# K Qᵀ and K S as one 112-column product, and two small products moved to other visits, in a DeltaNet + SwiGLU kernel

## The chip, the cores and the metric

The kernel runs on one core of one Trainium2 chip. The metric is the device time of one execution in microseconds, the median of several runs. The engines are TensorE (PE, with its weight loads listed as PEld), VectorE (DVE), ScalarE (ACT), GpSimd (POOL) and SyncE (SP), which issues most DMAs. All numbers are fp32.

## The reference

Two blocks follow each other. The first is a DeltaNet recurrence over 768 steps for 4 batches of 8 heads with a head dimension of 48; its output, 3072 rows of 384, goes through a SwiGLU feed-forward block with 1536 hidden columns.

```python
k_n = k / (norm(k) + 1e-6)
state = zeros(B, H, D, D)
for t in range(S):
    y[:, :, t] = einsum('bhd,bhde->bhe', q[:, :, t], state)
    v_old = einsum('bhde,bhd->bhe', state, k_n[:, :, t])
    state = state + beta[t] * einsum('bhd,bhe->bhde', k_n[:, :, t], v[:, :, t] - v_old)
x = y.transpose(0, 2, 1, 3).reshape(B * S, H * D)
g = x @ w_gate
out = (g * sigmoid(g) * (x @ w_val)) @ w_out
```

## The kernel before

The 768 steps are cut into 12 chunks of 64. Inside a chunk the recurrence is a handful of matrix products per head, with the state S (48 x 48 a head) carried from chunk to chunk. For chunk c they are, in order: the grams K Kᵀ and K Qᵀ (64 x 64 a head), r = V − K S, u = Z r with Z the inverse of a triangular matrix made from K Kᵀ, the new state S + Kᵀ u, and the output y = Q S + P u with P the masked K Qᵀ. The feed-forward block of chunk c runs while the recurrence of chunk c+1 is worked off between its products.

There are 32 heads (4 batches x 8). For each product TensorE runs 32 matmuls, one a head; `every()` walks over the heads so that four successive ones fall on the four 64x64 quadrants of the array: the row half by the head's parity `par`, the column half by the batch half `b` and `par`. Each matmul leaves two records in the trace (64 for a product). The results lie in two pairs of PSUM banks, `px` and `py`; the feed-forward products use four other banks, `ffn`.

All engines run in an order written out by hand. The feed-forward block of a chunk (`gate_val_fast`, three rounds, then `output_fast`) calls `point(c + 1)` at fixed places; each such visit does one thing for the recurrence: a step of `join`, a step of `products` (`turned`, that is the transposed K and Q, then in another visit the `gram`), or a step of `advance`. After a visit `fill(n)` gives VectorE some steps of the triangular inversion (`invert`) of a later pair of chunks, as many as fit in the budget n less what the visit has used up (`spent`). `finish` works off whatever is still due at the end of a chunk; `may_advance` says when a chunk's first step may be taken.

`advance(c)` for a chunk from 2 on has four steps, each a visit:

- the r visit: K S into `px` (L918), Q S into `py` (L927), then VectorE subtracts K S from V (L935);
- the u visit: u into `px` (L957), ScalarE copies it out (L969);
- the P u visit: Kᵀ u into `px` (L1025), VectorE adds it to the state (L1034), P u is added onto Q S in `py` (L1013), ScalarE copies y out (L1070, L1072);
- the transposes of y (L1086) and a copy to `x_ffn` (L1092).

The grams (L521) are made in a visit of their own: K Kᵀ in `px`, copied out by ScalarE (six copies, L547 and L550), K Qᵀ in `py`, masked by VectorE (L539). K runs some four chunks ahead of the recurrence, Q one chunk. From K chunk 6 and Q chunk 3 on, the transposes are done by VectorE (L494) from blocks that SP loads (`load_blocks`, L173).

Of the kernel before, what the change touches and what calls it, by code (L numbers as in the profile page):

```python
# [20 lines left out]
def kernel(  # L21
# [25 lines left out]
    nc = tc.nc  # L47

    B, H, S, D = q.shape
    NCH = S // C  # L50
    NJ = H // 2
    NB = B // 2
# [9 lines left out]
    const = ctx.enter_context(tc.tile_pool(name="const", bufs=1))  # L62
# [11 lines left out]
    def ps_pair(name, tag):  # L74

        return pairs_of_banks[tag]
# [35 lines left out]
    def kt_of(c):  # L112
        return kts[c] if c < AHEAD else kts_late[c % 4]
# [202 lines left out]
    nc.vector.memset(half, 0.5)  # L316

    spare = const.tile([128, 1], FP32, name="spare")
    nc.scalar.activation(spare, half[:, 0:1], ACTF.Silu)
# [154 lines left out]
    def banks(name, tag):  # L474

        if type(tag) is int:
            return [ps_ffn([128, 512], name, tag + i) for i in range(2)]
        p = ps_pair(name, tag)
        return [p[:, 0], p[:, 1]]

    def turned(c, of_q, tag=None):

        if tag is None:
            tag = "py" if of_q else "px"
        x = qpad[c % QB] if of_q else kn_of(c)
        if of_q:
            xt = work.tile([128, NB * NJ * 2 * C], FP32, name="qt", bufs=1)
        else:
            xt = kt_of(c)
        if c >= blocks_of[of_q][1]:  # L490
            xt_v = xt.rearrange("p (b bp j i) -> p bp j b i", bp=NB, b=2, j=NJ)
            (qt if of_q else kt)[c] = xt_v
            blocks = blocks_of[of_q][2]
            nc.vector.transpose(xt, blocks.rearrange("p bp h d -> p (bp h d)"))  # L494
# [4 lines left out]
        xt = xt.rearrange("p (bp j b i) -> p bp j b i", bp=NB, j=NJ, b=2)  # L499
        (qt if of_q else kt)[c] = xt  # L500
        p_t = banks("p_t", tag)
        for bp in range(NB):
            for j in range(NJ):
                at = slice(128 * j, 128 * j + 128)
                nc.tensor.transpose(p_t[bp][:, at], x[:, bp, 2 * j : 2 * j + 2], ident)
            if type(tag) is int:
                nc.scalar.copy(xt[:, bp].rearrange("p j b i -> p (j b i)"), p_t[bp])
        for bp in range(NB if type(tag) is not int else 0):
            nc.scalar.copy(xt[:, bp].rearrange("p j b i -> p (j b i)"), p_t[bp])
        if of_q and c + QB < Q_BLOCKS:  # L510
            load_q(c + QB)

# [42 lines left out]
    def gram(*args):  # L555
        for _ in gram_steps(*args):
            pass
# [348 lines left out]
    def advance(c):  # L906
# [4 lines left out]
        if c > 0 and c not in scaled:  # L911
            scale_v(c)
        r = vin.pop(c)
        if c > 0:
            p_y = recur(ps_pair("p_y", "py"))
            p_r = recur(ps_pair("p_r", "px"))
            for bp, j, par, b, first in every():
                nc.tensor.matmul(  # L918
                    p_r[half_of(b ^ par), par, bp, j],
                    kt[c][head_of(par), bp, j, b],  # L920
                    state[head_of(par), b, bp, j],
                    start=first,
                    stop=True,
                    skip_group_check=True,
                )
            for bp, j, par, b, first in every():
                nc.tensor.matmul(  # L927
                    p_y[half_of(b ^ par), par, bp, j],
                    qt[c][head_of(par), bp, j, b],
                    state[head_of(par), b, bp, j],  # L930
                    start=first,
                    stop=False,
                    skip_group_check=True,
                )
# [76 lines left out]
        def p_of_u():  # L1011
            for bp, j, par, b, _ in every():
                nc.tensor.matmul(  # L1013
                    p_y[half_of(b ^ par), par, bp, j],
                    pq[half_of(b), par, bp, j],
                    uu[half_of(b), par, bp, j],
                    start=False,
                    stop=True,
                    skip_group_check=True,
                )  # L1020
# [21 lines left out]
                    else:  # L1042
                        late_loads.append(lambda: load_k(c + 2))

        if 0 < c < NCH - 1:
            of_state()
        y = work.tile([128, NB, NJ, 2, D], FP32, name="y", tag="r", bufs=2)
        if c == 0:
            third = single(2)[0]
            for par in range(2):  # L1050
                for bp in range(NB):
                    p = third if par and bp else p_y[par]
                    for j in range(NJ):
                        for b in range(2):
                            nc.tensor.matmul(
                                p[half_of(b ^ par), bp, j],
                                pq[half_of(b), par, bp, j],
                                uu[half_of(b), par, bp, j],
                                start=j == 0 and (bp == 0 or par == 1),
                                stop=True,  # L1060
                                skip_group_check=True,
                            )
                if par == 0:
                    nc.scalar.copy(y[:, :, :, 0], p_y[0])
            for b in range(2):
                nc.scalar.copy(y[half_of(b), 0, :, 1], p_y[1][half_of(1 - b), 0])
                nc.vector.tensor_copy(y[half_of(b), 1, :, 1], third[half_of(1 - b), 1])
        else:
            p_of_u()
# [286 lines left out]
    def minus(out, a, b):  # L1356
        nc.vector.tensor_tensor(out=out, in0=a, in1=b, op=ALU.subtract)
# [159 lines left out]
    def steps(kind, *args):  # L1517
        return gens.get((kind, args), (None, 0))[1]

    fills = []  # L1520
    inverted, joined1 = set(), []

    def products(k_c, q_c):

        if k_c is not None:
            turned(k_c, False)
        if q_c is not None:
            turned(q_c, True)
        yield
        if k_c is not None:  # L1530
            gram(k_c, False, None, (nc.scalar.copy, nc.scalar.copy))
            if k_c % 2 == 1:
                fills.append((k_c // 2, invert(k_c // 2)))
        if q_c is not None:
            gram(q_c, True)
        yield
# [30 lines left out]
    def prep_step(c):  # L1567

        for g in range(1, c // 2 + 2):
            late = g == 1 and (  # L1570
                hold or steps("join", g) >= 2 and steps("advance", 2) < 4
            )
            if g in inverted and steps("join", g) < (4 if g == 1 else 2) and not late:
                step("join", join if g > 1 else join_1, *((g,) if g > 1 else ()))
                return True
        if going:
            next(going.pop())
            return True
# [8 lines left out]
        next(gen)  # L1587
        going.append(gen)
        return True

    def point_and_fill(c, n, fill):
# [208 lines left out]
```

## Time and profile before

| | |
|---|---|
| median of 3 runs | 698.48 us (698.16 to 700.41) |
| span of the profiled execution, first to last instruction | 694.1 us |
| median less span | 4.4 us |
| TensorE busy | 680.5 us, 98% |
| VectorE busy | 473.1 us, 68% |
| ScalarE busy | 259.8 us, 37% |
| mean granted TensorE clock | 0.997 |

The profile gives no device time of its own for the profiled execution, only the span; the median is 4.4 us above it, for what lies around the first and the last instruction. A line such as L918 is that line of the kernel before. In the timeline each row is a start, a length, the engine, the line and the operation, with the number of merged records; matmuls are pipelined, so the length of a group holds the drain of its last record, and what a group costs is read from the start of the next one.

### The profile page before, as it was taken

Reading aid. Unit: us, or ns where it says so; the run is one execution under the profiler, and the core shown is the slowest. Engines: PE = TensorE matmul, PEld = TensorE weight load, DVE = VectorE, ACT = ScalarE, POOL = GpSimd, SP = SyncE. Lnnn points to the kernel's source line nnn. Section 1 sums busy time; section 2 is a strip of 40 time slices with the busy share of each in tenths; the row PEclk is TensorE's granted clock in tenths of the full one; section 3 lists DMA queues with packets and bytes.
Section 4 is the critical chain, followed back from the end, with each engine's and each line's share of the span. In section 5 each row is a group of like instructions: output and inputs, shape, how many; then the busy total and the mean of one; then the engine's idle time right before and its main releaser. Section 6 shows DMA issues by size and latency. Waiting matters only on the chain.

```text
span 694.1 us, 25652 instructions
## 1 busy us (share of the span) xinstructions
PE 680.5 (98%) x11380; PEld 635.6 (92%) x11380; DVE 473.1 (68%) x1104; ACT 259.8 (37%) x549; POOL 53.5 (8%) x62
## 2 busy tenths in 40 slices
PE   8799999999999999999999999999999999999997
PEld 4688888757999999999999999999999999999997
DVE  6887779798899758896469786389844345333342
ACT  4674776214442532344233244242153142142230
POOL 5110031105000030000300002100000000000000
PEclk9999999999999999999999999999999999999999
DMA  9567924017550621564432363243241231221210
GB/s 136 148 167 180 275 69 161 1 34 174 133 109 16 117 79 40 103 116 84 94 72 70 73 135 70 56 108 70 55 108 48 58 83 46 55 63 46 69 47 23
DMA packets 143854, 62.31 MB, mean 90 GB/s; under 512 B 122976, under 2 KB 126048, under 8 KB 143744
## 3 DMA queue, kind: packets, MB, share of 16 engines
q1 hardware_dynamic: 141536, 60.19, 37.0%
q8 instruction: 89, 1.46, 0.9%
q10 hardware_dynamic: 2080, 0.39, 0.4%
q0 software_dynamic: 128, 0.10, 0.1%
q14 instruction: 21, 0.17, 0.1%
HBM read 53.58 MB, written 7.08 MB: 87 GB/s over the span
## 4 chain that ended last, share of the span: by engine, by line
PE 90%; DMA 4%; SPq 3%; ACT 1%; issue 1%; DVE 1%; POOL 0%; ACTq 0%; POOLq 0%; DVEq 0%
PE ffn L1193 43%; PE ffn L1399 20%; PE ffn L1289 8%; PE ffn L1316 4%; DMA h_f<-in_moe_w_val_dram 3%; PE p_px L957 2%; PE p_px L918 2%; PE p_py L1013 2%; SPq L140 1%; PE p_py L927 1%; PE p_py L521 1%; PE p_px L1025 1%; PE p_px L521 1%; SPq L186 1%; PE p_py L1086 1%; DMA wo_sb<-in_moe_w_gate_dram 1%
## 5 line engine op out<-in xcount | busy, mean ns | idle before, releaser
L1193 PE MATMUL ffn<-x_ffn,wg_sb 128*128 128x128 f32 x840 | 128.3, 275 | 0.3 <-ACT x_ffn L1092 0.2
L1193 PE MATMUL ffn<-x_ffn,wv_sb 128*128 128x128 f32 x840 | 128.1, 275 | 0.0
L1193 PEld LDWEIGHTS ffn<-x_ffn,wg_sb 128*128 128x128 f32 x840 | 111.1, 192 | 0.6 <-ACT ffn L1249 0.3
L1193 PEld LDWEIGHTS ffn<-x_ffn,wv_sb 128*128 128x128 f32 x840 | 110.7, 192 | 0.0
L1223 ACT ACTIVATE sil<-ffn 128x256 f32<-128x256 f32 x120 | 46.1, 384 | 131.8 <-PE ffn L1193 127.1
L1399 PE MATMUL ffn<-wo_sb,h_f 128*128 128x192 f32 x480 | 83.4, 327 | 0.0
L1228 DVE TENSOR_TENSOR h_f<-sil,ffn 128x256 f32<-128x256 f32 x120 | 49.5, 418 | 47.7 <-ACT sil L1223 45.2
L1399 PEld LDWEIGHTS ffn<-wo_sb,h_f 128*128 128x128 f32 x480 | 78.1, 190 | 0.4
L1360 DVE TENSOR_TENSOR ffn<-ffn,p_sb 128x512 f32<-128x512 f32 x58 | 40.4, 696 | 44.1 <-ACT ffn L1249 43.0
L1193 PE MATMUL ffn<-x_t,h_f 128*128 128x128 f32 x480 | 61.1, 280 | 0.0
L1193 PEld LDWEIGHTS ffn<-x_t,h_f 128*128 128x128 f32 x480 | 56.2, 191 | 1.4 <-ACT ffn L1206 0.2
L599 DVE TENSOR_TENSOR zb<-zb,tmp 128x31 f32<-128x31 f32 (+15 forms) x155 | 53.1, 342 | 5.3
L593 DVE TENSOR_TENSOR tmp<-zb,mb 128x31 f32<-128x31 f32 (+15 forms) x155 | 52.6, 339 | 4.0
L826 POOL TENSOR_TENSOR n_b<-mb,half 128x32 f32<-128x32 f32 x5 | 30.0, 6003 | 289.2 <-DVE mb L563 289.2
L1360 DVE TENSOR_TENSOR o_sb<-o_sb,ffn 128x192 f32<-128x192 f32 x49 | 17.2, 351 | 51.2 <-PE ffn L1399 49.1
L1206 ACT COPY ffn<-ffn 128x512 f32<-128x512 f32 x30 | 17.1, 571 | 63.5 <-PE ffn L1193 57.1
L1399 PE MATMUL ffn<-last_k,h_f 128*128 128x192 f32 x200 | 35.9, 327 | 0.0
L1289 PE MATMUL ffn<-x_ffn,wg_sb 128*128 128x256 f32 x144 | 34.4, 385 | 0.0
L1289 PE MATMUL ffn<-x_ffn,wv_sb 128*128 128x256 f32 x144 | 33.8, 382 | 0.0
L1399 PEld LDWEIGHTS ffn<-last_k,h_f 128*128 128x128 f32 x200 | 32.9, 190 | 0.0
L1289 PEld LDWEIGHTS ffn<-x_ffn,wg_sb 128*128 128x128 f32 x144 | 26.5, 190 | 4.3 <-DVE wg_sb L309 0.7
L1289 PEld LDWEIGHTS ffn<-x_ffn,wv_sb 128*128 128x128 f32 x144 | 27.0, 190 | 3.7
(302 smaller groups left out, 1064.3 us busy)
## 6 DMA issues: line engine op xcount, KB each, us to landing
h_f<-w_s SPq DMA_DIRECT2D x60, 256.0 KB, 2.9
p_sb<-w_s SPq DMA_DIRECT2D x27, 256.0 KB, 2.7
vin<-in_v_dram SPq DMA_DIRECT2D x48, 96.0 KB, 3.2
out_dram<-o_sb SPq DMA_DIRECT2D x48, 96.0 KB, 2.2
kn<-in_k_dram SPq DMA_DIRECT2D x20, 192.0 KB, 4.7
zt<-in_moe_w_out_dram SPq DMA_DIRECT2D x6, 384.0 KB, 3.7
qpad<-in_q_dram SPq DMA_DIRECT2D x36, 64.0 KB, 3.2
w_s<-h_f SPq DMA_DIRECT2D x7, 256.0 KB, 4.1
```

Source lines behind the costliest of these rows:

```text
L521: nc.tensor.matmul(p_v[par][half_of(b if of_q else b ^ par), bp, j], kt[c][half_of(par), bp, j, b], xt[half_of(par), bp, j, b],)
L593: nc.vector.tensor_tensor(out=t_v, in0=zb[:, 0 : j + 1, j : j + 1].to_broadcast([128, j + 1, m]), in1=mb[:, j : j + 1, j + 1 : R].to_broad ...
L599: nc.vector.tensor_tensor(out=zb[:, 0 : j + 1, j + 1 : R], in0=zb[:, 0 : j + 1, j + 1 : R], in1=t_v, op=ALU.add,)
L826: nc.gpsimd.tensor_tensor(out=n, in0=mb.rearrange("p j i -> p (j i)")[:, 0 : R * R : R + 1], in1=half, op=ALU.pow,)
L1193: nc.tensor.matmul(p[:, u], w(u), moving, start=start and u == 0, stop=True, skip_group_check=True,)
L1206: nc.scalar.copy(p_y, p_x)
L1223: nc.scalar.activation(sil[:, n].rearrange("p (i n) -> p i n", i=2), p[:, 0:2], ACTF.Silu)
L1228: nc.vector.tensor_tensor(out=h_of(c, f, j), in0=sil[:, n].rearrange("p (i n) -> p i n", i=2), in1=p[:, 2:4], op=ALU.mult,)
L1289: nc.tensor.matmul(ps[name][:, i], w_sb[:, t, (f + i) * 128 : (f + i + 1) * 128], xts[c][:, t], start=(t == 0 and i == 0), stop=(t == KT - 1),
L1316: nc.tensor.matmul(p_o, hs[c, f - f % 2][:, f % 2, bp * 128 : (bp + 1) * 128], wo_sb[:, f], start=(f == 0), stop=(f == FT - 1),)
L1360: nc.vector.tensor_tensor(out=out, in0=a, in1=b, op=ALU.add)
L1399: nc.tensor.matmul(p[x, part], a(f - f % 2)[:, f % 2], b(f), start=not begun and f == 0, stop=f == FH - 1, skip_group_check=True,)
```

## The change

From chunk 4 on (`FUSED = 4`) Q is turned into the same tile as the state: `qs` has 16 slots of 112 columns, 64 of Qᵀ and 48 of the state. The r visit then makes K Qᵀ and K S in one product of 112 moving columns with Kᵀ stationary; a head's parity decides whether it lands in `px` or `py`. VectorE takes K S off V in two halves and masks K Qᵀ in three pieces. Q S is made at the beginning of the P u visit; behind it ScalarE copies two elements of its result to `spare_2`. K Kᵀ of chunks 7 to 11 (`K_LATE = 7`) is made in `py` in the u visit of whichever chunk comes next. The visits that held only grams are gone from chunk 4 on; `may_advance` asks for the turned Q instead of the masked P. Before chunk 4 the products stay as they were, with the state and Qᵀ now views of `qs`.

```diff
-    state = const.tile([128, 2, NB, NJ, D], FP32, name="state")
+    qs = const.tile([128, B * NJ, C + D], FP32, name="qs")
+    state = qs[:, :, C : C + D].rearrange("p (b bp j) d -> p b bp j d", b=2, bp=NB)
+    q_part = qs[:, :, 0:C].rearrange("p (b bp j) i -> p bp j b i", b=2, bp=NB)
+    FUSED, K_LATE = 4, 7
+    waiting_k = []
...
+            if of_q:
+                qt[c] = q_part
+                nc.vector.transpose(
+                    qs[:, :, 0:C], blocks.rearrange("p (h i) -> p h i", i=C)
+                )
...
+        if c >= FUSED:
+            both = [
+                [p.rearrange("p (j n) -> p j n", j=NJ) for p in row]
+                for row in (
+                    [bank[:, 0 : NJ * (C + D)] for bank in banks("p_r", tag)]
+                    for tag in ("px", "py")
+                )
+            ]
+            for bp, j, par, b, _ in every():
+                nc.tensor.matmul(
+                    both[par][bp][half_of(b ^ par), j],
+                    kt[c][head_of(par), bp, j, b],
+                    qs[head_of(par), NB * NJ * b + NJ * bp + j],
+                )
...
+            for par in range(2):
+                minus(r[:, par], r[:, par], pair[par][:, :, :, C : C + D])
...
+            for to, of, par in (
+                (slice(0, 128), slice(0, 128), 0),
+                (half_of(0), half_of(1), 1),
+                (half_of(1), half_of(0), 1),
+            ):
+                rows = of.stop - of.start
+                nc.vector.tensor_tensor(
+                    out=p_sb[c][to, par],
+                    in0=pair[par][of, :, :, 0:C],
+                    in1=mask_q[of, None, None, :].to_broadcast([rows, NB, NJ, C]),
+                    op=ALU.mult,
+                )
+            spent.append(3.3)
+            yield
+        elif c > 0:
...
         uu = v0
+        if c >= FUSED and waiting_k:
+            k_gram(waiting_k.pop(), "py")
...
-        if 0 < c < NCH - 1:
+        if 0 < c < FUSED:
             of_state()
...
         else:
+            if c >= FUSED:
+                p_y = recur(ps_pair("p_y", "py"))
+                q_of_state(p_y)
+                nc.scalar.copy(spare_2, p_y[:, :, 0, 0, 0:1])
+                if c < NCH - 1:
+                    of_state()
             p_of_u()
...
+        if k_c is not None and k_c >= K_LATE:
+            waiting_k.append(k_c)
+            k_c = None
+        if q_c is not None and q_c >= FUSED:
+            q_c = None
+        if k_c is None and q_c is None:
+            return
         yield
...
-        return steps("advance", c) > 0 or (c in p_sb and steps("join", g) >= due)
+        ready = c in qt if c >= FUSED else c in p_sb
+        return steps("advance", c) > 0 or (ready and steps("join", g) >= due)
```

`q_of_state` is the old loop over L927 as a function, `k_gram` the old call of `gram` for K with the start of its inversion.

More of the change, by code (lines that the diff above doesn't have):

```diff
@@ L318 @@
     spare = const.tile([128, 1], FP32, name="spare")
+    spare_2 = const.tile([128, 2, 1], FP32, name="spare_2")
     nc.scalar.activation(spare, half[:, 0:1], ACTF.Silu)
@@ L485, in turned @@
         x = qpad[c % QB] if of_q else kn_of(c)
[L486 to L489, printed above, removed]
+        xt = None if of_q else kt_of(c)
         if c >= blocks_of[of_q][1]:
[L491 to L494, printed above, removed]
+            blocks = blocks_of[of_q][2].rearrange("p bp h d -> p (bp h d)")
+            if of_q:
[3 more added lines that the diff above has]
+                )
+            else:
+                kt[c] = xt.rearrange("p (b bp j i) -> p bp j b i", bp=NB, b=2, j=NJ)
+                nc.vector.transpose(xt, blocks)
             spent.append(1.8)
@@ L498, in turned, with copy_turned @@
             return
-        xt = xt.rearrange("p (bp j b i) -> p bp j b i", bp=NB, j=NJ, b=2)
+        if of_q:
+            xt = q_part
+        else:
+            xt = xt.rearrange("p (bp j b i) -> p bp j b i", bp=NB, j=NJ, b=2)
         (qt if of_q else kt)[c] = xt
         p_t = banks("p_t", tag)
+        def copy_turned(bp):
+            if of_q:
+                p = p_t[bp].rearrange("p (j b i) -> p j b i", j=NJ, b=2)
+                nc.scalar.copy(xt[:, bp], p)
+            else:
+                nc.scalar.copy(xt[:, bp].rearrange("p j b i -> p (j b i)"), p_t[bp])
         for bp in range(NB):
@@ L506, in turned @@
             if type(tag) is int:
-                nc.scalar.copy(xt[:, bp].rearrange("p j b i -> p (j b i)"), p_t[bp])
+                copy_turned(bp)
         for bp in range(NB if type(tag) is not int else 0):
-            nc.scalar.copy(xt[:, bp].rearrange("p j b i -> p (j b i)"), p_t[bp])
+            copy_turned(bp)
         if of_q and c + QB < Q_BLOCKS:
@@ L913, in advance, with q_of_state @@
         r = vin.pop(c)
-        if c > 0:
+        def q_of_state(p):
+            for bp, j, par, b, first in every():
+                nc.tensor.matmul(
+                    p[half_of(b ^ par), par, bp, j],
+                    qt[c][head_of(par), bp, j, b],
+                    state[head_of(par), b, bp, j],
+                    start=first,
+                    stop=False,
+                    skip_group_check=True,
+                )
[8 more added lines that the diff above has]
+            for bp, j, par, b, _ in every():
+                nc.tensor.matmul(
+                    both[par][bp][half_of(b ^ par), j],
+                    kt[c][head_of(par), bp, j, b],
+                    qs[head_of(par), NB * NJ * b + NJ * bp + j],
+                )
+            pair = [
+                ps_pair("p_r", tag)[:, :, 0 : NJ * (C + D)].rearrange(
+                    "p bp (j n) -> p bp j n", j=NJ
+                )
+                for tag in ("px", "py")
+            ]
+            for par in range(2):
+                minus(r[:, par], r[:, par], pair[par][:, :, :, C : C + D])
+            p_sb[c] = p_places[1].rearrange(
+                "p (x bp j i) -> p x bp j i", x=2, bp=NB, j=NJ
+            )
+            for to, of, par in (
[9 more added lines that the diff above has]
+                    op=ALU.mult,
+                )
+            spent.append(3.3)
+            yield
+        elif c > 0:
             p_y = recur(ps_pair("p_y", "py"))
@@ L925, in advance @@
                 )
[L926 to L934, printed above, removed]
+            q_of_state(p_y)
             nc.vector.tensor_tensor(out=r, in0=r, in1=p_r, op=ALU.subtract)
@@ L1068, in advance @@
         else:
+            if c >= FUSED:
+                p_y = recur(ps_pair("p_y", "py"))
+                q_of_state(p_y)
+                nc.scalar.copy(spare_2, p_y[:, :, 0, 0, 0:1])
+                if c < NCH - 1:
+                    of_state()
             p_of_u()
@@ L1521, with k_gram @@
     inverted, joined1 = set(), []
+    def k_gram(c, tag=None):
+        gram(c, False, tag, (nc.scalar.copy, nc.scalar.copy))
+        if c % 2 == 1:
+            fills.append((c // 2, invert(c // 2)))
     def products(k_c, q_c):
@@ L1528, in products @@
             turned(q_c, True)
+        if k_c is not None and k_c >= K_LATE:
[5 more added lines that the diff above has]
+            return
         yield
         if k_c is not None:
-            gram(k_c, False, None, (nc.scalar.copy, nc.scalar.copy))
-            if k_c % 2 == 1:
-                fills.append((k_c // 2, invert(k_c // 2)))
+            k_gram(k_c)
         if q_c is not None:
@@ L1586, in prep_step @@
         gen = products(k_c, q_c)
-        next(gen)
-        going.append(gen)
+        if next(gen, MORE) != MORE:
+            going.append(gen)
         return True
```

## The prediction

> **What bounds the kernel now.** I read the page's first part and its chain of waits, then the table by stage, then the order of TensorE's instructions around single visits, then the costs of single evictions.
>
> ```profile
> PE 680.5 (98%) x11380; PEld 635.6 (92%) x11380; DVE 473.1 (68%) x1104; ACT 259.8 (37%) x549; POOL 53.5 (8%) x62
> PE 90%; DMA 4%; SPq 3%; ACT 1%; issue 1%; DVE 1%; POOL 0%; ACTq 0%; POOLq 0%; DVEq 0%
> ```
> ```profile
> 390.00:440.00 50.00, 50.00 (x1031) 48.88 (x1026) 36.41 (x79) 20.05 (x42) 6.33 (x2) 1.00 0.47 93
> 490.00:540.00 50.00, 49.85 (x972) 48.52 (x972) 28.14 (x64) 17.49 (x35) 0.00 (x0) 1.00 0.29 73
> ```
> In the second fence (window, its length, then busy time of PE, PEld, DVE, ACT, POOL, then the granted clock) TensorE is busy for all of 50 us, or all but 0.15, at a clock of 1.00. So wherever the change works (chunk 4 on, some 240 us to 620 us) the time is the sum of what TensorE has to run; VectorE has a quarter or more of each stretch free, ScalarE more than half. A microsecond of TensorE work saved there is one of the total, until a new wait eats it.
>
> What the attention visits cost TensorE is read from starts in the timeline (start, length, instruction; x64 are records, two to a matmul):
>
> ```profile
> 419.55 0.61 PE L1193 MATMUL ffn<-x_ffn,wv_sb 128*128 128x128 f32 x4
> 420.09 1.16 PE L521 MATMUL p_px<-kn 64*64 64x64 f32 x64
> 421.07 1.11 PE L521 MATMUL p_py<-qt,kt 64*64 64x64 f32 x64
> ...
> 443.60 0.61 PE L1193 MATMUL ffn<-x_ffn,wv_sb 128*128 128x128 f32 x4
> 444.14 1.15 PE L918 MATMUL p_px<-state,kt 48*64 48x48 f32 x64
> 445.11 1.11 PE L927 MATMUL p_py<-state,qt 48*64 48x48 f32 x64
> 446.15 2.05 PE L1193 MATMUL ffn<-x_t,h_f 128*128 128x128 f32 x16
> ...
> 457.45 0.94 PE L1025 MATMUL p_px<-uu,kn 64*48 64x48 f32 x64
> ```
> Each group of 32 products takes about 0.97 us from its start to the next group's, with 64 moving columns (L521) as with 48 (L918). Only L1025, whose stationary operand has 48 columns instead of 64, is shorter: 0.75 us (458.20 - 457.45). So these products are bound by loading their stationary columns, not by streaming. The records' single starts say the same: four start 7 ns apart, on the four quadrants, and the next four follow 58 ns after the first ones (L521 with 64 columns and L957 with 48 alike), 45 ns after in L1025. That is what the change can use: more moving columns under the same weight loads.
>
> **The change, part by part.** TensorE first, chunks 4 to 11. A visit's cost is from the end of the feed-forward unit before it (its start plus 0.447, the step between units) to the start of the next.
>
> Removed: the visits with K K^T and K Q^T, 422.11 - 420.00 = 2.11 us each (chunk pairs 7/4, 8/5, 9/6, 10/7, 11/8: five), and those with K Q^T alone (chunks 9, 10, 11): 475.51 - 474.33 = 1.18 us, three. Together 14.1 us. Also the eight visits with K S and Q S, 446.15 - 444.05 = 2.10 us each: 16.8 us. Sum 30.9 us.
>
> Added: (a) K K^T of chunks 7 to 11 behind the product that makes u, in the u visit: 0.97 us each, 4.85 us, the entry into the visit being paid already. (b) Q S ahead of K^T u and P u: 0.97 us, eight times, 7.76 us. (c) Eight products of 112 columns, 32 matmuls each. No row has this shape; the bounds are these. Below, the weight loads alone, 0.97 us. Above, two groups one after the other, 1.94 us; more than that, say only two quadrants streaming at once, is excluded, since 64 records of 64 columns (60.7 ns each by the slope below) would then take 1.94 us in L521, which takes 0.97. How long a record of 112 columns streams: a unit of 4 records at 128 columns steps by 0.447 us (111.7 ns each), 12 records at 192 by 1.95 us (162.6 ns each), so 0.80 ns a column and 98.9 ns at 112. The nearest row for whether four quadrants stream at once is L446 (16x32 stationary, 192 columns, at 10.66 us): its 16 records start in four bursts of four, 7 to 14 ns apart inside a burst, the bursts at 10.665, 10.852, 11.014 and 11.177. The last steps are 162 to 163 ns, one full stream, so four run at once and their weight loads hide. I take that: 16 rounds of 98.9 ns are 1.58 us, plus 0.04 us that a group needs beyond its rounds now (0.97 against 16 x 58 ns); with 0.16 us of entry and exit (2.10 - 2 x 0.97) the visit costs 1.78 us, eight times 14.2 us.
>
> Sum: 4.85 + 7.76 + 14.2 = 26.8 us against 30.9: **-4.1 us** of TensorE work.
>
> A rule speaks against it. The Trainium skill, "TensorEngine Tiling (Array Packing)", Instruction Overhead, says that a matmul carries about 60 cycles of overhead, so one with few columns lasts as long as one with 60. By it 48 + 64 columns cost as 60 + 64, and 112 instead saves only a tenth of 1.94 us: the product is 1.75 us, and the sum -3.1 us (an estimate from that page). The trace does not bear it out: L1025 streams the same 48 columns in 0.75 us.
>
> VectorE: before, L935 (953 ns for 768 elements) and two L539 (680 ns for 512) make 2.3 us a chunk. After, two subtractions of 384 (0.55 us by L1360's 351 ns for 192 and 696 for 512) and three maskings of 512 (two on 64 partitions), 3.1 us: +0.8 us a chunk, +6.6 us in all, and now in one visit. Its cover is the free quarter of VectorE: the next product that touches these banks is u, one visit later, 4.66 us after the fused product ends (446.15 to 450.82 now). In the tightest place, chunks 5, 7 and 9, where the fused product comes at the start of a chunk behind a fill of five steps, the timeline of the same place now (272 to 295 us) has VectorE at those fills until 285.5; there I get 286.9 for the last eviction of px and 288.1 for py, against u at 288.0 and K K^T into py at 289.0: about 1 us to spare. Nothing is charged; without that cover it would be what VectorE is late, three times.
>
> The queue of fills is no longer than before: in the order of the changed kernel no chunk is forced ahead, and each join still comes before its chunk's first step. The transposes of K and Q keep their place behind the last step of a chunk; the visit where their gram stood is now empty. SP's block loads move up by one half round in two places (8 issues take 5.0 us, landing takes 3.1 us); they still land 1 us before the transposes.
>
> The waits added. P u (PE) now waits for a two-element ScalarE copy that reads the Q S banks; it is there eight times. Behind it on TensorE stands everything. Q S's last record ends 0.22 us after its group; ScalarE starts about 0.04 us later (281.68 to 281.72 in L1206), a copy that small is some 0.18 us by extrapolating L1423 (321 ns for 192) and L1249 (572 ns for 512), and 0.06 us back: 0.5 us, beside K^T u's 0.75 us. Hidden, if ScalarE is free, seven times; chunk 11 has no K^T u, so 0.5 us there. In chunks 4, 6 and 8 ScalarE may not be free. The u visit there also makes K K^T, whose six copies take 2.72 us (L547, L550); VectorE then stands waiting for them with its two transposes (L563, 2.19 us), behind these the gating multiply of p_y, for which the last Silu waits, and behind that the small copy. Counted from the start of u: copies until 4.9, transposes until 7.1, multiply 7.5, Silu 7.9, clear 8.2, copy 8.4; K^T u ends at 8.42. It just fits; I charge 0.1 us each, 0.3 us, with a bound of 2 us each. Before the change that order did not exist, so a gain is excluded here.
>
> Total -4.1 + 0.5 + 0.3 = -3.3 us, and down to -3.7 if a record of 112 columns has only the 2.5 ns over its stream that L446 shows (95.8 instead of 98.9 ns). I take **-3.5 us** against the profiled span of 694.1. The median of the runs, 698.48, lies 4.4 us above that span, which the change doesn't touch: 698.48 - 3.5 = 695.0.
>
> **The rivals.** (1) *The fused product streams without full overlap.* At 1.94 us, the price of two groups, the sum loses 8 x 0.32 = 2.6 us: 697.6, no change that can be told. For it: no 64x64 product in the trace streams more than 64 columns. Against: L446's bursts. (2) *A floor per matmul, not the weight load, sets the 0.97 us of 48 columns:* then 112 columns save little over 48 and 64, 1.75 us instead of 1.62, eight times, +1.0 us: 696.0. Against: L1025. This is the overhead rule of the Trainium skill's tiling page as it would work here. (3) *Slower: the small ScalarE copy is late.* It decides from where ScalarE comes more than 1.9 us late to it in the three chunks 4, 6 and 8 (3.5 + 2.1 us over three); if VectorE's transposes and one more queued step come in front, 3 us each, 9 us: 704. For it: my count has no slack there. Against: the order puts only 0.4 us more work into that queue than I counted. (4) *More gain,* 693.5: the empty visits drop more entry cost than 0.16 us.
>
> **How the numbers follow.** What can be told from no change here is 0.3%, about 2.1 us. Forecast 0.65, all of it faster; (1) 0.13, all of it within 0.3%; (2) 0.05, faster; (3) 0.09, slower; (4) 0.08, faster. Faster 0.78, same 0.13, slower 0.09. The range goes from (4) to (1), 693.3 to 697.6, and leaves out (3) and a little at each end.
>
> **What would show it.** In the changed profile: the fused rows (32 matmuls of 64x112, on px and py in turn) with 1.55 to 1.65 us from first start to next unit; no separate visit of the gram after chunk 4; the first unit after a u visit with K K^T 0.97 us later than without; VectorE's total up by 6 to 7 us, TensorE's busy time down by 4; no idle time of TensorE over 0.2 us in front of P u but 0.5 us in chunk 11. The prediction is wrong if the fused product takes 1.9 us or more, if P u's wait stands before chunks 4, 6, 8 with over 1 us, or if u waits for the maskings.

## The result, and the profile after: slower, not faster

The changed kernel takes 703.02 us (median of 4 runs, 702.66 to 705.33) against 698.32 us for the kernel before beside it (4 runs, 697.64 to 700.41): ratio 1.0069, 95% interval 1.0045 to 1.0094. Forecast was 695.0. The work on TensorE fell as forecast; 8.2 us of new stops ate that and left 4.4 us on top.

The page, first part and chain of waits, of the changed kernel:

```profile
PE 682.3 (97%) x10868; PEld 636.0 (90%) x10868; DVE 476.1 (68%) x1120; ACT 260.7 (37%) x557; POOL 54.2 (8%) x62
PE 82%; DVE 12%; issue 3%; ACT 2%; DMA 1%; SPq 0%; DVEq 0%; ACTq 0%
```

512 matmul records fewer, as the change says. But the chain, 1% VectorE before, is now 12% VectorE and 3% "issue", time in which the engine waited for nothing that the profile shows. The table by stage (window, length, busy time of PE, PEld, DVE, ACT, POOL, granted clock) shows VectorE's work bunched:

```profile
340.00:390.00 50.00, 47.99 (x956) 46.80 (x955) 22.81 (x43) 19.02 (x40) 6.34 (x2) 1.00 0.29 69
390.00:440.00 50.00, 49.85 (x732) 49.04 (x731) 44.88 (x112) 16.61 (x37) 0.24 (x1) 1.00 0.53 104
440.00:490.00 50.00, 49.33 (x964) 47.78 (x963) 27.93 (x60) 19.36 (x42) 4.73 (x1) 1.00 0.24 66
490.00:540.00 50.00, 49.83 (x675) 48.89 (x674) 41.00 (x101) 14.49 (x32) 1.85 (x3) 1.00 0.48 97
```

The stages have moved by some microseconds between the kernels, so the windows don't hold the same work; still, VectorE is busy for 23, 45, 28 and 41 us of 50 in turn, where the same windows showed 36, 36, 40 and 28. Over the whole run its busy time is nearly the same (476.1 against 473.1 us).

The fused product, from the timeline of TensorE (start, length, instruction):

```profile
285.49 0.61 PE L1262 MATMUL ffn<-x_ffn,wv_sb 128*128 128x128 f32 x4
286.03 0.31 PE L953 MATMUL p_px<-qs,kt 48*64 48x112 f32 x1
286.03 0.31 PE L953 MATMUL p_py<-qs,kt 48*64 48x112 f32 x1
...
286.17 0.26 PE L953 MATMUL p_px<-qs,kt 48*64 48x112 f32 x1
...
286.27 0.26 PE L953 MATMUL p_px<-qs,kt 48*64 48x112 f32 x1
...
287.72 0.71 PE L1262 MATMUL ffn<-x_t,h_f 128*128 128x128 f32 x4
```

Four records start together, the next four 0.14 us later and each further four after 0.10 us (96 ns): all four quadrants stream at once. From the first start to the next unit it is 1.69 us (287.72 - 286.03).

The first new stop, in chunk 5's visit of P u, from the timeline of all engines:

```profile
300.59 0.52 PE L935 MATMUL p_py<-qs 48*64 48x48 f32 x23
300.93 0.90 PE L1088 MATMUL p_px<-uu,kn 64*48 64x48 f32 x64
301.18 0.16 ACT L1135 COPY spare<-p_py 128x2 f32<-128x2 f32 x1 [0.54 <-PE p_py L935]
301.65 1.10 PE L1076 MATMUL p_py<-uu,p_sb 64*64 64x48 f32 x60
304.05 0.32 PE L1076 MATMUL p_py<-uu,p_sb 64*64 64x48 f32 x4 [1.29 <-issue]
```

The small copy (L1135) ends at 301.34, before P u begins. P u runs 60 of its 64 records and then stops, four records from its end, with no operand missing: 1.5 us pass between two records (1.4 us by the measure of the table below). The waits of TensorE (engine, line, released by: us in total, times, longest):

```profile
PEld p_py L1076 <- issue: 4.3, 4, 1.5
PEld ffn L1468 <- DVE o_sb L1429: 2.9, 5, 0.9
PEld ffn L1262 <- DVE ffn L1429: 1.4, 3, 0.7
PEld p_py L913 <- issue: 0.8, 1, 0.8
PE p_py L1076 <- ACT spare L1135: 0.3, 1, 0.3
```

To compare the kernels I add up one number from each trace: the time from the first product of chunk 2 (line of `product4`) to the start of TensorE's last record. It leaves out what differs between executions at the start: that first product came between 170.1 and 178.2 us in the fourteen profiles, in no relation to the kernel (172.1 before, 177.2 after, 178.2 in an experiment that is faster than the changed kernel). So about 5 us of the 9.5 us between the two profiled spans are not the change's: in the changed kernel's profile the granted clock from 13 to 49 us was 0.81, in that of before 0.95 from 13 to 45. A "stop" is a gap of over 0.3 us between the starts of two matmul records, less the 0.11 us of one record; "rest" is the length without stops.

| kernel | length | stops in rows of small products | stops in feed-forward products | rest |
|---|---|---|---|---|
| before | 517.60 | 0 | 0.32 | 517.28 |
| **changed** | 522.01 | 4.62 | 3.85 | 513.53 |
| x1_split | 523.33 | 1.97 | 4.53 | 516.84 |
| x2_outfill | 553.38 | 10.50 | 19.65 | 523.22 |
| x4_kown | 521.71 | 4.87 | 1.85 | 514.99 |
| x5_layout | 517.29 | 0 | 0.32 | 516.97 |
| x6_noqs | 510.49 | 1.28 | 4.10 | 505.11 |
| x13_quiet | 521.95 | 5.75 | 3.41 | 512.79 |
| x8_ktu2 | 525.91 | 2.78 | 0.32 | 522.82 |
| x9_ktu3 | 543.03 | 11.77 | 1.10 | 530.16 |
| x10_u2 | 524.13 | 0 | 0.32 | 523.81 |
| x7_qs_in_u | 516.50 | 0.56 | 1.44 | 514.50 |
| x11_copies | 517.99 | 0.92 | 2.65 | 514.42 |
| x12_two | 519.71 | 0.83 | 1.68 | 517.20 |

The length grows by 4.4 us, the median by 4.7. Inside it: TensorE's work -3.7; 4.2 us of stops named "issue" (3.5 in P u, 0.8 in a join); 0.4 us behind the small copy in chunk 11; 3.5 us more stops in feed-forward products.

### The profile page after: what moved, and what is told of

It reads as the page before. It is cut to its first block, busy times and chain, and to the rows that moved or that the text cites. A ratio compares the mean times of both kernels' runs of the same rounds, so it can differ in the third digit from the quotient of the medians.

```text
span 703.6 us, 24647 instructions
## 1 busy us (share of the span) xinstructions
PE 682.3 (97%) x10868; PEld 636.0 (90%) x10868; DVE 476.1 (68%) x1120; ACT 260.7 (37%) x557; POOL 54.2 (8%) x62
## 4 chain that ended last, share of the span: by engine, by line
PE 82%; DVE 12%; issue 3%; ACT 2%; DMA 1%; SPq 0%; DVEq 0%; ACTq 0%
PE ffn L1262 35%; PE ffn L1468 15%; PE ffn L1358 9%; PE ffn L1385 4%; DVE zb L617 3%; DVE tmp L611 3%; PE p_px L1018 2%; PE p_py L935 2%; PE p_py L1076 2%; PE p_px L953 1%; PE p_px L1088 1%; PE ffn L1040 1%; PE p_py L539 1%; PE p_px L1040 1%; DVE ffn L1429 1%
## 5 line engine op out<-in xcount | busy, mean ns | idle before, releaser
L1262 PEld LDWEIGHTS ffn<-x_ffn,wv_sb 128*128 128x128 f32 x840 | 110.7, 192 | 0.0
L1429 DVE TENSOR_TENSOR ffn<-ffn,p_sb 128x512 f32<-128x512 f32 x58 | 40.2, 694 | 39.8 <-ACT ffn L1318 38.8
L1429 DVE TENSOR_TENSOR o_sb<-o_sb,ffn 128x192 f32<-128x192 f32 x49 | 16.8, 347 | 52.8 <-PE ffn L1468 40.5
L1262 PE MATMUL ffn<-x_ffn,p_sb 128*128 128x128 f32 x216 | 30.1, 282 | 0.6 <-DVE ffn L1429 0.5
```

What stands on the lines that cost most here:

```text
L1262: nc.tensor.matmul(p[:, u], w(u), moving, start=start and u == 0, stop=True, skip_group_check=True,)
L1429: nc.vector.tensor_tensor(out=out, in0=a, in1=b, op=ALU.add)
```

## The experiments

Two theories. **A**: TensorE runs out of fetched instructions. In the trace its instructions arrive on a queue of their own, in pieces of 16384 bytes, 85 of them in the run of the changed kernel and 89 before. The pages count 21736 and 22760 records of PE and PEld together (2 x 10868 and 2 x 11380), so a piece is 256 instructions. A group of 32 matmuls is 128 (64 loads, 64 products). All three stops in P u and the one in the join end 1.2 to 1.4 us after such a piece has landed (piece 301.60 to 302.69, stop until 304.05; 378.26 to 379.41, until 380.83; 588.55 to 589.80, until 591.17; 355.82 to 356.78, until 357.98). Counted along TensorE's records in the trace, the four instructions that waited stand 1280, 1024 and 6656 places apart, whole multiples of 256, as the first instructions of pieces would. **B**: with the gram visits gone, visits without a step hand their whole budget to VectorE's fills, which bunch ahead of what the output products wait for. Rivals: **C**, the small ScalarE copy; **D**, the new layout itself.

### x1_split: P u in a visit of its own

```diff
                 if c < NCH - 1:
                     of_state()
+                yield MORE
             p_of_u()
```


> The changed kernel with one edit: the visit of P u is cut in two. Q S and K^T u stay in one visit, P u comes in the next one. No operation is added or left out; 384 TensorE instructions in a row (3 groups of 32 matmuls, each matmul a load and a product in two passes) become 256 and 128 with feed-forward products between. Theory A (TensorE runs out of fetched instructions in the long rows): the stops inside P u (1.51, 1.56, 0.74 us in the profile, 4.2 us in all) go, eight more entries into a visit come at 0.16 us (1.3 us): 700.1 against 703.0. Theory B (VectorE's fills make the output products late, 2 to 3 us; P u's stops are something else): the stops in P u stay, 703 to 704. Theory C (the small ScalarE copy ahead of P u is what P u waits for): the stops go and the wait of 0.5 in chunk 11 goes too.

702.72 us (ratio to before 1.0082, 1.0052 to 1.0112): no gain. The stops in P u are gone, all of them, but the extra point of each chunk pushed other steps on. Waits of TensorE:

```profile
PE ffn L1263 <- ACT x_ffn L1162: 2.9, 4, 0.9
PE p_px L953 <- DVE qs L496: 1.8, 1, 1.8
```

In chunks 6, 8 and 10 the last step, the transposes of y, now falls to `finish`, with nothing between it and the chunk's first product (1.05 us of stop each), and once the fused product waits 2.0 us for the transpose of Q. Of the other 3.3 us in "rest" 1.3 are the eight entries; the remainder I did not break down. So A's local claim held, the sum did not: a place in the order is itself a cost.

### x2_outfill: no fills between the output products

```diff
-            fill(2)
             product_3()
             plus(o[1][:, right], o[0][:, right], p[1, 0])
-            fill(2)
 ...
-        fill(5)
+        fill(9 if c > FAST else 5)
```


> The changed kernel with one edit: the two fills (VectorE steps of the inversion) that are given out in the middle of a chunk's output products are moved behind its last product, from chunk 3 on; the total of fills is the same. Theory B (these fills stand ahead of VectorE's additions and differences, for which the output products wait): the waits of the output products for VectorE, 0.97, 0.97, 0.47 and 0.33 us in chunks 4, 6 and 8, go: 700.3 to 700.8 against 703.0; if the moved steps make the next chunk's first products late instead, 702 to 703. Theory A: P u's stops of 4.2 us stay in this run, whatever else it does; a gain of over 3 us would speak against A.

733.53 us (ratio 1.0512, 1.0481 to 1.0543), far off. The waits in the output products went, all of them; the moved steps came back dearer, since a budget of 9 in one lump, by the planner's costs in microseconds, stands ahead of the next chunk's first additions:

```profile
PE ffn L1262 <- DVE ffn L1429: 11.9, 6, 3.4
PE p_py L1076 <- issue: 6.9, 5, 2.3
```

That VectorE's place in the order is what counts is borne out, my price for moving it is not: 30 us.

### x4_kown: K K^T back in visits of its own

```diff
-    FUSED, K_LATE = 4, 7
+    FUSED, K_LATE = 4, 12
```


> The changed kernel with one edit: K K^T of chunks 7 to 11 stays in a visit of its own, as it was before the change; the fused product and Q S in the visit of P u remain. TensorE work by the rows: five visits at 1.18 us in place of 0.97 us, +1.0 us. Theory A: the u visit falls from 256 instructions in a row to 128 ahead of the 384 of P u, so P u's stops get shorter, by 1 to 3 us: 701 to 703. Theory C (VectorE waits 4.1 us three times for the copies of K K^T in chunks 4, 6 and 8, and this makes what is behind it late): these waits go from the small copy's chain; 700 to 701. If neither counts, 704.

701.86 us (ratio 1.0059, 1.0036 to 1.0081), which the time alone doesn't tell from the changed kernel's 1.0069; the stops do. TensorE's work rose by 1.5 us, and the feed-forward stops fell from 3.85 to 1.85, those in the output products from 2.55 to 0.55: with K K^T earlier the fills start earlier and spread. Of the 1.85 us that are left 0.8 aren't VectorE's: two stops (350.27 and 446.44 us) end 1.5 and 1.4 us after a piece of instructions has landed. P u's stops stayed (3.5 and 3.1 us, so 128 instructions fewer one visit earlier don't matter). For B; against C, whose ScalarE chain was undone here without touching them.

### x5_layout: the layout alone

```diff
-    FUSED, K_LATE = 4, 7
+    FUSED, K_LATE = 12, 12
 ...
-        if 0 < c < FUSED:
+        if 0 < c < NCH - 1:
             of_state()
```


> The changed kernel with the change switched off for all chunks (first fused chunk 12, first late K K^T 12): only the layout remains, Q^T and the state in one tile of 112 columns for each head, and ScalarE's and VectorE's writes into it in strides. Every product is that of the kernel before. Theory D (the layout costs something of its own, in the first 50 us above all, where the profile of the changed kernel is 4.2 us behind): 700 to 702. If it costs nothing: 698.3, as the kernel before, and the 4.2 us at the start are the lower clock of that one execution.

697.87 us against 697.41 for the kernel before on the same chip (ratio 1.0017, 0.9997 to 1.0037); length 517.29 against 517.60. D is out.

### x8_ktu2, x9_ktu3, x10_u2: longer rows in the kernel before

```diff
-            for bp, j, par, b, first in every():
+            for _, (bp, j, par, b, first) in [
+                (n, e) for n in range(2 if c >= 4 else 1) for e in every()
+            ]:
                 nc.tensor.matmul(
                     p_s[
```
(x9 has 3 for 2; x10 has the same loop of 2 around u, from chunk 4 to 10.)

> The kernel before the change, with K^T u of chunks 4 to 10 made twice in the same place: 384 TensorE instructions in a row in the P u visit where there were 256; nothing else changes. The second making costs 7 x 0.75 = 5.3 us. Theory A: stops inside P u or at the end of K^T u, as in the changed kernel some 0.5 us a visit, 3.5 us in all, on top: 8.8 us more than the kernel before. Without A (the stops came from the changed kernel's small copy or its banks): 5.3 us more and no stop.

> As the run before, K^T u made three times: 512 instructions in a row. 10.5 us of work. Theory A: pieces of 256 instructions arrive 3.5 us apart at best and the row takes 3.3 us, so the stop grows to about 1.5 us a visit, 10 us in all: 20 us more than the kernel before. Without A: 10.5 us more.

> The kernel before the change, with u of chunks 4 to 10 made twice in the u visit: 128 instructions in a row become 256, and the row of 256 in the P u visit stays. 7 x 0.97 = 6.8 us of work. Theory A with its limit above 256: no stop, 6.8 us more than the kernel before. If stops come as in the run with 384, what counts is the number of instructions over some microseconds and not the row.

Against 698.54 us on that chip: 706.89, 724.38 and 705.39 us (ratios 1.0127, 1.0377, 1.0105; intervals within 0.004). No small copy, no fused product and no new order is in these kernels, and stops appear with the length of the row: none at 256, in three of seven visits at 384, in seven of seven at 512. The same chunk in the timelines of x8 and x9:

```profile
304.26 1.66 PE L1027 MATMUL p_px<-uu,kn 64*48 64x48 f32 x128
305.74 0.51 PE L1013 MATMUL p_py<-uu,p_sb 64*64 64x48 f32 x19
307.21 0.91 PE L1013 MATMUL p_py<-uu,p_sb 64*64 64x48 f32 x45 [0.96 <-issue]
```
```profile
307.81 2.37 PE L1027 MATMUL p_px<-uu,kn 64*48 64x48 f32 x192
310.01 0.51 PE L1013 MATMUL p_py<-uu,p_sb 64*64 64x48 f32 x19
312.51 0.90 PE L1013 MATMUL p_py<-uu,p_sb 64*64 64x48 f32 x45 [1.99 <-issue]
```

Work added is 5.5, 12.9 and 6.5 us, the rest is stops: 2.8, 11.8 and 0. x8 and x10 came out as A said (8.4 us for 8.8, 6.9 for 6.8); x9 cost 25.8 us for 20: its work is 2.4 us over the price, its stops 1.8 us, and 0.8 us came among the feed-forward products. I had worked out the stops from the spacing of pieces (3.4 us at least). What the trace shows is the delay: from the start of a piece's transfer to TensorE's going on it is 2.2 to 2.8 us (304.77 to 307.21 in x8, 309.72 to 312.51 in x9), and a row uses 256 instructions in 1.5 to 1.9 us.

Why only some rows of 384 stop can be counted in the traces: what decides is where the edges of the pieces fall. Over all profiles, from chunk 2 on, a piece's transfer starts about when TensorE begins the piece before it (0.7 us after, as the median of some 900 pieces), so a piece that is run through in less than 2.2 to 2.8 us finds the next one missing. Of the 35 rows of 384 (the changed kernel, x2, x4, x8, x13) 16 hold a whole piece and the first instruction of the next, and these 16 stop; the other 19 do not. A row of 512 always holds one, a row of 256 cannot: where one stopped all the same, in joins, a piece had begun 12 to 38 instructions ahead of it.

### x6_noqs and x13_quiet: one cost of the changed kernel taken out

```diff
                 p_y = recur(ps_pair("p_y", "py"))
-                q_of_state(p_y)
-                nc.scalar.copy(spare_2, p_y[:, :, 0, 0, 0:1])
```
(and P u starts its banks itself), x13:
```diff
+            quiet.append(1)
             fill(2)
             product_3()
             plus(o[1][:, right], o[0][:, right], p[1, 0])
             fill(2)
+            quiet.clear()
```
(where `quiet` is set, `turn` and `substitute` issue nothing.)

> The changed kernel in its own order, with Q S of chunks 4 to 11 (8 x 32 matmuls) and the small ScalarE copy behind it left out, so the output lacks Q S there; the P u visit has 256 TensorE instructions in a row in place of 384. Work left out: 8 x 0.97 = 7.8 us, and 0.5 us of the copy in chunk 11. Theory A: the stops in P u (3.5 us in the changed kernel's profile) and the one in a join (0.8 us) go besides, 703.0 - 7.8 - 0.5 - 4.2 = 690.5, and the waits of the output products for VectorE (2.5 us) stay, since no VectorE work is touched. Without A: 694.7, with stops of over 0.5 us left in P u.

> The changed kernel in its own order, with the substitution steps and the two transposes of 128x512 that fall into the middle of the output products of chunks 4, 6 and 8 left out (about 2.4 us of VectorE work in each; the inverses of these groups are not complete then). No TensorE work changes. Theory B: the waits of the output products for VectorE there (0.97 and 0.33 us, 0.97 and 0.35, 0.47) go, 2.5 us, and P u's stops stay: 700.5 against 703.0. If VectorE is only named and something else holds the products, 703.

x6: 690.85 us, 690.5 expected. No stop in P u from chunk 4 on, and the waits of the output products are what they were (2.54 for 2.55 us in all); the stop in a join did not go (1.28 us): joins are rows of 256 with other visits close by, and can stop too. x13: 700.94 us for 700.5 (ratio to before 1.0049, 1.0021 to 1.0077, where the changed kernel had 1.0069 on another chip; the intervals overlap, so the time alone doesn't show the gain, the waits do). The output products of chunk 4 in the changed kernel and in x13:

```profile
334.52 1.57 PE L1468 MATMUL ffn<-last_k,h_f 128*128 128x192 f32 x8
335.92 0.81 PE L1468 MATMUL ffn<-last_h,h_f 128*128 128x192 f32 x4
337.38 0.92 PE L1468 MATMUL ffn<-wo_sb,h_f 128*128 128x192 f32 x4 [0.65 <-DVE o_sb L1429]
```
```profile
335.11 1.46 PE L1474 MATMUL ffn<-last_k,h_f 128*128 128x192 f32 x8
336.41 0.81 PE L1474 MATMUL ffn<-last_h,h_f 128*128 128x192 f32 x4
337.06 2.11 PE L1474 MATMUL ffn<-wo_sb,h_f 128*128 128x192 f32 x12
```

In the first the last line comes 1.46 us after the one before it, in the second 0.65; in between VectorE of the changed kernel was at fills (L581, L870, L875; the two rows of L581 are among what x13 leaves out):

```profile
332.24 2.03 DVE L581 STREAM_TRANSPOSE zt<-zb 128x512 f32<-128x512 f32 x2
334.16 0.31 DVE L1429 TENSOR_TENSOR o_sb<-o_sb,ffn 128x192 f32<-128x192 f32 x1
334.39 0.76 DVE L870 STREAM_TRANSPOSE z<-zt 128x256 f32<-128x256 f32 x2
335.18 0.76 DVE L875 STREAM_TRANSPOSE z<-zt 32x256 f32<-32x256 f32 x2
335.97 1.10 DVE L1426 TENSOR_TENSOR h_f<-h_f,h_f 128x256 f32<-128x256 f32 x3
336.98 0.61 DVE L1429 TENSOR_TENSOR o_sb<-o_sb,ffn 128x192 f32<-128x192 f32 x2
```

The additions into o_sb (L1429), which free the banks, stand behind the transposes. No such wait is left in x13. Its length is still 521.95: P u's stops were 1.1 us longer in that execution, and ten of its output products ran at half the clock:

```profile
378.00:382.00 4.00, 2.11 (x96) 1.94 (x85) 1.94 (x4) 0.55 (x2) 4.00 (x1) 1.00 0.04 9
382.00:386.00 4.00, 4.00 (x16) 4.00 (x16) 0.00 (x0) 1.49 (x4) 1.30 (x2) 0.57 0.02 4
```

The granted clock (third number from the right) falls to 0.57 right after a stop of 2.1 us in P u. That happened in this profile alone; whether the stop is its cause is open.

### x7_qs_in_u, x12_two, x11_copies: the fused product without its price

x7 puts Q S behind u, where only u stands, and K K^T in visits of its own: no row over 256, fills as early as before.
```diff
-        if c >= FUSED and waiting_k:
-            k_gram(waiting_k.pop(), "py")
+        if c >= FUSED:
+            p_y = recur(ps_pair("p_y", "py"))
+            q_of_state(p_y)
+            nc.scalar.copy(spare_2, p_y[:, :, 0, 0, 0:1])
 ...
-            if c >= FUSED:
-                p_y = recur(ps_pair("p_y", "py"))
-                q_of_state(p_y)
-                nc.scalar.copy(spare_2, p_y[:, :, 0, 0, 0:1])
-                if c < NCH - 1:
-                    of_state()
+            if FUSED <= c < NCH - 1:
+                of_state()
```


> The fused product kept, with Q S put behind u in the u visit (256 TensorE instructions in a row) in place of the P u visit, and K K^T of chunks 7 to 11 in visits of their own as before the change, so that the inversion's fills start as early as before and no visit has 384 in a row. TensorE work against the kernel before: 16.8 + 14.1 us taken out, 5 x 1.18 + 8 x 0.97 + 14.0 = 27.7 us put in, -3.2 us. Theory A and B together (the changed kernel lost to long rows and to bunched fills alone): no stop in P u, none over 0.4 us in the output products, 695 where the kernel before has 698. Theory A alone: the stops in P u go, waits for VectorE of 2 to 3 us stay, 697.5. If Q S now waits for the maskings of the fused product (VectorE), TensorE stands ahead of Q S by 1 us or more in some chunks: 697 to 699.

x12 is x7 with the 112 columns made as two products:
```diff
-                    both[par][bp][half_of(b ^ par), j],
+                    both[par][bp][half_of(b ^ par), j, C : C + D],
                     kt[c][head_of(par), bp, j, b],
-                    qs[head_of(par), NB * NJ * b + NJ * bp + j],
+                    qs[head_of(par), NB * NJ * b + NJ * bp + j, C : C + D],
                 )
+            (the same loop again, with columns 0:C)
```


> The version with Q S behind u and K K^T in visits of its own, with the product of 112 columns made as two products of 48 and 64 columns into the same banks, in one visit: what the fusing by itself brings. By the rows 1.94 us in place of 1.69, eight times: 2.0 us more than that version, the time of the kernel before. If four quadrants did not stream at once with 112 columns, no difference.

x11 is x7 with one half of the copies of K K^T (the two small ones of that half too) on VectorE:
```diff
-        gram(c, False, tag, (nc.scalar.copy, nc.scalar.copy))
+        gram(c, False, tag, (nc.scalar.copy, nc.scalar.copy if c < K_DVE else nc.vector.tensor_copy))
```


> The version with Q S behind u and K K^T in visits of its own, with one edit: of the six copies of K K^T (chunks 7 to 11) the three of the second half go from ScalarE to VectorE, which in these visits no longer has the maskings of K Q^T. Two stops of 0.44 us behind ScalarE's four copies (2.6 us) in front of the next feed-forward product go: 0.9 us less than that version, 2.8 us less than the kernel before, if VectorE's 1.5 us more at that place stay hidden; if not, no gain or 0.5 us more.

x7: 696.65 us against 698.54, ratio 0.9984 (0.9963 to 1.0006), where the changed kernel has 1.0069 (1.0045 to 1.0094): better than the change, and not told apart from the kernel before. Its chain is TensorE again:

```profile
PE 94%; ACT 2%; DVE 2%; issue 2%; DVEq 0%; ACTq 0%
```

"Rest" is 2.8 us below the kernel before (3.2 expected), stops are 1.7 us above it: two of 0.33 us behind ScalarE's copies of K K^T, two of 0.56 and 0.34 us that end 1.2 and 1.4 us after a piece of instructions has landed, 0.2 us at VectorE, and 0.2 us at the place where the kernel before has 0.3. x12: ratio 1.0035 (1.0010 to 1.0060); rest 2.7 us above x7, eight times 0.33: two products take 2.03 us where one takes 1.69. The fusing is worth that, as much as the whole 2.8 us by which x7's rest is below the kernel before. x11: 1.0014 (0.9990 to 1.0038), a miss: the two stops behind ScalarE went, but VectorE was not free at that place, and the output products wait for it again (0.8 us). The other part is not VectorE's: in a join and at 350.3 us two stops that end 1.5 and 1.6 us after a piece has landed are 0.9 and 1.0 us, where x7 has 0.6 and less than 0.2.

## Why the prediction was wrong

**TensorE's work: right.** -4.1 us forecast, -3.7 measured; the fused product took 1.69 us, 1.62 forecast (rounds of 96 ns, 95.8 to 98.9 forecast, and 0.15 us beyond them instead of 0.04, at the first round and the end). Rival 1 (no overlap, 1.94 us) is out by that time; rival 2 (a floor per matmul, 1.75 us) is as near to it as the forecast and is out by x12, which shows 2.7 us between one product and two, where the floor would have left 8 x 0.19 = 1.5 us.

**The waits that I added: right, and small.** Chunk 11's copy cost 0.4 us (0.5 forecast). In chunks 4, 6 and 8 ScalarE's chain cost nothing at P u (0.3 charged). Rival 3 gave 704, close to the time, by this copy; the profile puts 0.3 us on it, once. A right time from a wrong mechanism.

**First failing step: a term that wasn't in the sum.** I priced Q S at 0.97 us "ahead of K^T u and P u" as if a group cost the same wherever it stands. It made three groups in a row, 384 instructions, and from chunk 2 on the trace of before has no row longer than 256 without feed-forward work. It cost 4.2 us of stops: the 3.5 us in P u go with Q S (x6) and come with the length of the row in the kernel before (x8 to x10); the 0.8 us in the join did not go with Q S (1.3 us in x6); it stands at a piece's edge like the others. The Trainium skill, "Runtime: NRT & Kernel Launch", Instruction fetch mechanics, says that instructions come through a small FIFO refilled in 16 KiB blocks of 256, and that the fetch is hidden because the sequencer issues more slowly than the blocks fill. The block size agrees with the trace (16384 bytes); the hiding does not hold here, with stops of 0.4 to 2.4 us that end 1.2 to 1.6 us after a block lands. The rows of before already carried the warning, which I did not read: K S and Q S of one visit ahead of chunk 2's first product, 256 instructions in a row, stop three records from their end, 1.4 us after a piece has landed.

```profile
161.15 1.14 PE L927 MATMUL p_py<-state,qt 48*64 48x48 f32 x61
162.57 0.32 PE L927 MATMUL p_py<-state,qt 48*64 48x48 f32 x3 [0.29 <-issue]
```

**Second failing step: "Nothing is charged" for VectorE, and "the queue of fills is no longer than before".** The length of the queue was right and beside the point. `point_and_fill` gives a visit its budget less what the step spent, so an empty visit, which I mentioned only for its entry cost, gives all of it. And K K^T waits for the u visit of the next chunk: for chunk 7 it starts 84.9 us after the first product of chunk 2 instead of 55.2, and the inversion behind it 88.9 instead of 67.2 (66.7 in x4). In chunk 4 of the changed kernel VectorE is at nothing but the inversion from 321.59 to 324.97 us and from 327.13 to 331.70, while the output products run from 324.60 on; in the kernel before, that inversion is through at 314.3 us but for one pair of transposes, and the output products start at 320.57. It cost 3.5 us of stops, shown by x13 (2.5 us go with the fills) and by x4 (2.0 us go with the earlier K K^T). x4 fills five of the emptied visits again and brings the start back, so how much of it the empty visits make, and how much the later start, no run separates. VectorE's total rose by 3.0 us, 6 to 7 forecast; I had looked at its sum and at one eviction's slack, not at who stands behind a bunch.

**The sum:** -3.7 + 0.4 + 4.2 + 3.5 = +4.4 us; the medians say +4.7. (The range begins at 693.3, 0.2 us below the 693.5 of the rival that it is taken from.) Of the signs that I named, fused rows of 1.55 to 1.65 us were nearly met, TensorE's busy time did not fall by 4 (680.5 to 682.3; the profile after had a lower clock at the start), and "no idle time over 0.2 us in front of P u" was met to the letter while the stops stood inside P u. None of the events that I said would prove it wrong came: the list held only waits for operands.

## What to carry to other kernels

Cost a moved product by its row: count the instructions of small products that now follow each other without longer work between, and keep them to less than one piece of instructions (256 here). Beyond that it is a matter of where the pieces' edges fall, and these move with every edit ahead of the row. Splitting or moving one group can be worth more than the fusing gained. When a change empties a slot of an order that is filled by budget, ask which work flows into the slot, and what on that engine then comes late; a queue of the same length in another place is another queue. A place in the order is a cost too: the split that cured the stops (x1) lost the gain by pushing the last step to the end of the chunk.

## What the runs showed of the hardware that I had not expected

TensorE's instructions come in pieces of 256; from the start of a piece's transfer (about 1.0 us long) to the first instruction run from it 2.2 to 2.8 us pass where TensorE stops for it, and a row of small products at 130 to 170 instructions a microsecond outruns that wherever it holds a whole piece (16 of 35 rows of 384, all seven of 512), while 256 ran through in u and P u, though not always in a join (stops of 0.6 to 1.4 us). Two products of 48 and 64 columns with the same stationary operand cost 0.33 us more than one of 112 (2.03 against 1.69 us for 32). The start of the kernel, to the first product of chunk 2, varied by 8 us between executions, whatever the kernel, so that single spans say little about a change of a few microseconds.
